# Attention, mixture of experts and FFN on one core: a third PSUM bank for the down products, a shorter 64-bit decode, and side work moved inside the units

## The chip, the cores and the metric

The kernel runs on 1 core of one Trainium2 chip. The metric is device microseconds of an execution, the median of several runs; lower is better. Before the change it is 2050.29 us (median of 3 runs, 2049.09 to 2053.37).

## The reference, cut to what matters

```python
# attention: 4 batches, 8 heads, 576 positions, head_dim 64
scores = where(mask, q @ k.T / 8, -1e9)       # heads 0-3: last 32 keys, heads 4-7: every 32nd key
x = softmax(scores) @ v                       # -> 2304 tokens x 512
# mixture of experts, E = 8, F = 1024: every token goes through every expert
P = exp(x @ w_gate - max); 8 rounds of row and column normalisation (Sinkhorn)
x = sum_e P[:, e] * (relu(x @ w1[e]) @ w2[e])
# FFN: 512 -> 2048 -> 512; its weights reach the chip as 64-bit numbers
h = x @ w_in;  out = (h * sigmoid(1.702 * h)) @ w_out
```

## The kernel before, in words

**Units.** The 2304 tokens are 3 blocks of 768 (2 x 384). A unit is one block with 256 of the hidden columns: 32 units a block in the mixture (8 experts x 4), 8 a block in the FFN, 120 in all, numbered 0 to 119. Units 0 to 31 are block 0 of the mixture, 32 to 95 blocks 1 and 2, 96 to 119 the FFN. Attention runs in front of and between units 0 to 9.

**Products.** The up product of a unit is a Strassen-like scheme of 7 products (the table `PRODUCTS`, called k = 0 to 6 here), each of 6 matmuls of 384 columns, since each fp32 factor is split into a high and a low part (high*high + high*low + low*high). Product k=0 opens PSUM bank A; 2, 4 and 6 go on adding into it; 1 opens bank C and 5 adds into it; 3 opens bank B. `product_and_after` hangs work on each: ScalarE copies A and C (line 820), VectorE adds a copy to a bank (lines 849 and 868; the one at 868 reads A after k=4, so k=6, which adds into A, has to wait for it). From the sums come the four quadrants of the hidden tile. In block 0, `activate` makes a high part on ScalarE (830) and a low part on VectorE (833). In blocks 1 and 2, `scaled` multiplies by the gate's rows on VectorE (910), with a high part on ScalarE (899) and a low part on VectorE or GpSimd (904).

**Down products.** Between two up products stands one down product of the unit (or pair of units) before. In block 0 and the FFN it is `tile_down`: 6 matmuls of 512 columns into a bank `y`, drained by VectorE into `acc` (1066 to 1072, 1080, 1082). Its first tile of a unit needs the quadrants 11 and 12 of the unit before, and 12 comes out of the late product k=5. In blocks 1 and 2 it is `chain`: 6 matmuls of 384 columns into `y`, drained by VectorE into `sum` (965, 967). `y` has two banks; so have A, B and C from unit 8 on (the lists `late` and `turn_of` in `open_bank`).

**Pieces.** The order is written out by hand. A unit is 13 pieces: up products at even ones, down products at odd ones. `side[g]` holds functions that are issued behind piece g; `spread` lays a list evenly over a range of pieces. All engines and the DMA queue of SyncE take their work in that order. Side work is:
- splits of weights into high and low parts (`split_into`: high on ScalarE at 236, low at 230 on VectorE or GpSimd, then a store so that later blocks can load them), with offsets in pieces for the low part and the store
- sums of weight quarters for the scheme: of w1 on GpSimd (215 to 217), of w2 in `plan_down_sums` (304), in line on GpSimd, or `again` on VectorE for the units before the late stage, whose w2 is loaded a second time (`raws`, line 313)
- at block changes the low parts of the next block's inputs (`input_low`, 499) and `join_sums` (988), which puts seven sums together to a block's result
- `decode`: 64 chunks of 64-bit weights, each a load, eight VectorE operations (419 to 428), one on GpSimd and a store, spread over units 34 to 90
- `plan_ahead`: splits of the first FFN units, in units 69 to 91, from one buffer `ws` with the parts `raw`, `sums` and `kw`.

At unit 32 the pool of block 0's weights is closed and `load_rows` (891) fetches the gate's rows for block 1.

## Time and profile before

| | |
|---|---|
| median of 3 runs | 2050.29 us |
| the profiled execution's own time | 2049.3 us |
| its span, first to last instruction | 2047.5 us |
| TensorE (PE) busy | 1972.0 us, 96% |
| PE weight loads | 1803.3 us, 88% |
| VectorE (DVE) | 1673.2 us, 82% |
| GpSimd (POOL) | 1202.5 us, 59% |
| ScalarE (ACT) | 817.4 us, 40% |
| DMA, HBM read and written | 383.99 and 161.53 MB, mean 268 GB/s |

PE's matmuls are pipelined and the ends of their records are modelled: one of 384 columns reads as 339 ns, while they start much closer together. So the busy share of PE hides short waits. What a stretch lost is better read from the number of its matmuls and the distance at which they start where nothing waits.

### The profile page before, as it was taken

Reading aid. Unit: us, or ns where it says so; the run is one execution under the profiler, and the core shown is the slowest. Engines: PE = TensorE matmul, PEld = TensorE weight load, DVE = VectorE, ACT = ScalarE, POOL = GpSimd, SP = SyncE. Lnnn points to the kernel's source line nnn. Section 1 sums busy time; section 2 is a strip of 40 time slices with the busy share of each in tenths; the row PEclk is TensorE's granted clock in tenths of the full one; section 3 lists DMA queues with packets and bytes.
Section 4 is the critical chain, followed back from the end, with each engine's and each line's share of the span. In section 5 each row is a group of like instructions: output and inputs, shape, how many; then the busy total and the mean of one; then the engine's idle time right before and its main releaser. Section 6 shows DMA issues by size and latency. Waiting matters only on the chain.

```text
span 2047.5 us, 33968 instructions
## 1 busy us (share of the span) xinstructions
PE 1972.0 (96%) x10865; PEld 1803.3 (88%) x10865; DVE 1673.2 (82%) x3077; ACT 817.4 (40%) x2040; POOL 1202.5 (59%) x1166
## 2 busy tenths in 40 slices
PE   8999989999999999999999999999998999999999
PEld 6777778888888899999999998989898989888887
DVE  6777688899987799999998799999997676666656
ACT  6555434545554333333333323323232335533432
POOL 4443356776877576676667767777676756800200
PEclk9999999999999999999999999999999999999999
DMA  6457588999997888988888788988888866665663
GB/s 235 137 206 243 173 277 320 366 353 344 368 350 247 285 293 289 292 288 284 281 268 286 249 300 278 297 295 301 307 303 285 273 215 229 246 229 180 211 192 127
DMA packets 294497, 547.80 MB, mean 268 GB/s; under 512 B 30672, under 2 KB 75952, under 8 KB 293040
## 3 DMA queue, kind: packets, MB, share of 16 engines
q1 hardware_dynamic: 294032, 545.18, 78.2%
q8 instruction: 87, 1.43, 0.3%
q14 instruction: 90, 0.74, 0.1%
q10 hardware_dynamic: 288, 0.46, 0.1%
HBM read 383.99 MB, written 161.53 MB: 266 GB/s over the span
## 4 chain that ended last, share of the span: by engine, by line
PE 64%; DVE 20%; DMA 8%; issue 3%; POOL 2%; ACT 2%; SPq 0%; DVEq 0%; ACTq 0%; POOLq 0%
PE pA L794 16%; PE y L957 14%; PE pC L794 8%; PE y L1055 6%; PE y L1053 6%; PE y L1054 6%; PE pB L794 4%; DVE r L910 2%; DVE comb L904 2%; DMA w<-s1moe 2%; DVE sum L967 2%; DMA s7moe<-kw 1%; PE sc L570 1%; DMA w<-s7moe 1%; DMA s2ffn<-ws 1%
## 5 line engine op out<-in xcount | busy, mean ns | idle before, releaser
L794 PE MATMUL pA<-xc,w 128*128 128x384 f32 x2880 | 581.7, 339 | 14.6 <-DVE pB L868 9.6
L957 PE MATMUL y<-comb,w 128*128 128x384 f32 x2688 | 547.8, 339 | 21.3 <-DVE sum L967 19.9
L794 PEld LDWEIGHTS pA<-xc,w 128*128 128x128 f32 x2880 | 511.0, 190 | 35.5 <-DVE pB L868 14.7
L957 PEld LDWEIGHTS y<-comb,w 128*128 128x128 f32 x2688 | 472.7, 189 | 38.8 <-DVE sum L967 36.4
L904 POOL TENSOR_TENSOR comb<-s,comb 128x384 fp32r<-128x384 f32 x256 | 285.8, 1127 | 217.7 <-ACT comb L899 210.5
L794 PE MATMUL pC<-xc,w 128*128 128x384 f32 x1464 | 297.5, 338 | 0.0
L899 ACT ACTIVATE comb<-r 128x384 fp32r<-128x384 f32 x192 | 100.9, 526 | 451.5 <-DVE r L910 418.1
L1053 PE MATMUL y<-w,hh 128*128 128x512 f32 x672 | 269.3, 401 | 9.0 <-DVE acc L1072 4.8
L1055 PE MATMUL y<-w,hl 128*128 128x512 f32 x672 | 270.1, 402 | 7.3 <-DVE hl L833 7.1
L967 DVE TENSOR_TENSOR sum<-y,sum 128x384 f32<-128x384 f32 x420 | 229.9, 548 | 51.9 <-PE y L957 50.9
L794 PEld LDWEIGHTS pC<-xc,w 128*128 128x128 f32 x1464 | 259.1, 188 | 9.8 <-issue 0.7
L1054 PE MATMUL y<-w,hh 128*128 128x512 f32 x672 | 267.2, 398 | 0.0
L230 POOL TENSOR_TENSOR w<-raw,w 128x512 fp32r<-128x512 f32 (+1 forms) x100 | 117.6, 1180 | 155.3 <-ACT w L236 136.8
L820 ACT ACTIVATE c<-pA 128x384 f32<-128x384 f32 x236 | 115.0, 487 | 184.4 <-PE pA L794 182.2
L1055 PEld LDWEIGHTS y<-w,hl 128*128 128x128 f32 x672 | 127.1, 189 | 42.1 <-DVE hl L833 14.1
L1053 PEld LDWEIGHTS y<-w,hh 128*128 128x128 f32 x672 | 127.5, 190 | 32.9 <-ACT hh L830 6.4
L929 POOL TENSOR_TENSOR s<-r,r 128x384 f32<-128x384 f32 x126 | 138.2, 1117 | 11.7 <-DVE r L910 11.7
L1082 DVE TENSOR_TENSOR acc<-y,acc 128x512 f32<-128x512 f32 x126 | 86.4, 686 | 69.8 <-PE y L1055 69.4
L794 PE MATMUL pB<-xc,w 128*128 128x384 f32 x708 | 142.8, 336 | 0.0
L1054 PEld LDWEIGHTS y<-w,hh 128*128 128x128 f32 x672 | 127.4, 190 | 15.5
L899 ACT ACTIVATE comb<-s 128x384 fp32r<-128x384 f32 x256 | 131.4, 513 | 7.8 <-POOL s L929 7.1
L794 PEld LDWEIGHTS pB<-xc,w 128*128 128x128 f32 x708 | 125.0, 188 | 4.9 <-issue 0.3
(155 smaller groups left out, 2987.7 us busy)
## 6 DMA issues: line engine op xcount, KB each, us to landing
w<-s1moe SPq DMA_DIRECT2D x448, 256.0 KB, 4.8
w<-s7moe SPq DMA_DIRECT2D x448, 256.0 KB, 4.7
s1moe<-w SPq DMA_DIRECT2D x216, 256.0 KB, 4.8
w<-s1ffn SPq DMA_DIRECT2D x133, 256.0 KB, 2.8
s7moe<-kw SPq DMA_DIRECT2D x128, 256.0 KB, 4.9
s7moe<-w SPq DMA_DIRECT2D x96, 256.0 KB, 3.8
w<-s2ffn SPq DMA_DIRECT2D x38, 512.0 KB, 4.1
raw<-wa SPq DMA_DIRECT2D x32, 512.0 KB, 6.1
```

Source lines behind the costliest of these rows:

```text
L230: eng.tensor_tensor(out=t[:, 1, :], in0=src, in1=f(t[:, 0, :]), op=ALU.subtract)
L794: nc.tensor.matmul(out=o, lhsT=w[:, hw, kk * P : (kk + 1) * P], rhs=x[:, hx, kk, :], start=opens and m == 0, stop=ends and m == len(todo) - 1,
L820: nc.scalar.activation(out=t, in_=bank[b][:, :NH], func=AF.Copy)
L899: nc.scalar.activation(out=t[:, 0, :], in_=part[i, q], func=AF.Copy)
L904: eng.tensor_tensor(out=t[:, 1, :], in0=part[i, q], in1=f(t[:, 0, :]), op=ALU.subtract)
L929: g.tensor_tensor(out=part[i, q], in0=part[i, a], in1=part[i, b], op=op)
L957: nc.tensor.matmul(out=o, lhsT=t[:, hw, dt * P : (dt + 1) * P], rhs=x[:, hx, :], start=(n == 0), stop=(n == 5))
L967: nc.vector.tensor_tensor(out=a, in0=o, in1=a, op=ALU.add)
L1053: nc.tensor.matmul(out=y, lhsT=hh[:, c], rhs=w[:, 0], start=(m == 0), stop=False)
L1054: nc.tensor.matmul(out=y, lhsT=hh[:, c], rhs=w[:, 1], start=False, stop=False)
L1055: nc.tensor.matmul(out=y, lhsT=hl[:, c], rhs=w[:, 0], start=False, stop=(m == 1))
L1082: nc.vector.tensor_tensor(out=a, in0=y, in1=a, op=ALU.add)
```

## The change

- `open_bank`: bank C keeps one bank in the late stage; the freed one is a third bank for the down products (`down_bank`), used every third time.
- `split_w1`: the low part of k=6's weights is issued 5 pieces behind its high part (was 1), the store 7 (was 3). `split_w2`: low part 2 or 1 pieces later (was 0), store 4 (was 2).
- `plan_down_sums`: sums in line at pieces 3, 3, 4, 5 (were 6, 6, 7, 7), in unit 31 at 0, 1, 1, 2; `again` at pieces 5 to 8 (were 8 to 11); splits at 6 to 9, in unit 31 at 4 to 7 (were 8 to 11), `again` at 0 to 3 of the next unit (were 0, 2, 4, 6). Nine units are done `again`, in units 11, 13, ... 27 (were eight, in 10 to 26).
- `decode`: without the operations at 421 and 427.
- `scaled`: the low part of quadrant 12 goes to GpSimd in all units of blocks 1 and 2 (was: in every second).
- block changes: three of the `input_low` in two halves, a piece or two later; `join_sums` in halves, in another order, one of them moved to GpSimd, the first already in the unit before.
- `plan_ahead`: parts rotate through `kw` and `sums`; the low part 1 piece behind the high one, stores 3 (were 0 and 4).
- the pools for blocks 1 and 2 are opened 4 pieces earlier.

```diff
-        if late and turn_of[b] % 2:
-            pool, tag = late[0], b + "2"
-        elif not late and i % 2:
+        if late:
+            if b != "C" and turn_of[b] % 2:
+                pool, tag = late[0], b + "2"
+        elif i % 2:
+    def down_bank(name):
+        turn_of["y"] += 1
+        if late and turn_of["y"] % 3 == 0:
+            return late[0].tile([P, D], F32, tag="y3", name=name)
+        return ps.tile([P, D], F32, tag="y", name=name, bufs=2)
...
-            split_into(t, src, kept, nc.vector, 1, 3)
+            split_into(t, src, kept, nc.vector, *((5, 7) if PRODUCTS[k][0] == "X22" else (1, 3)))
...
-                t = r["kw"].rearrange("p (h c) -> p h c", h=2)
+                t = r["kw"] if ft == 0 else r["sums"].rearrange("p q c -> p (q c)")
+                t = t.rearrange("p (h c) -> p h c", h=2)
...
-            lambda: v.scalar_tensor_tensor(xb, lo, 29, xb, ALU.logical_shift_right, ALU.bitwise_or),
...
-            lambda: v.tensor_scalar(lo, lo, 0x1FFFFFFF, None, ALU.bitwise_and),
...
-                put(last, 2 * m - 1, input_low, ph, m, v if m in low_v else g)
+                if m in low_v:
+                    put(last, 2 * m, input_low_half, ph, m, 0, v)
+                    put(last, 2 * m + 1, input_low_half, ph, m, 1, v)
+                else:
+                    put(last, 2 * m - 1, input_low, ph, m, g)
...
-            low_part(i, q, nc.gpsimd if q == "12" and (i - S0) % 2 == 0 else nc.vector)
+            low_part(i, q, nc.gpsimd if q == "12" else nc.vector)
...
-        y = ps.tile([P, D], F32, tag="y", name="y7", bufs=2)
+        y = down_bank("y7")
...
-        while done[0] < piece_at(S0 - 1, 7):
-            advance()
-        while done[0] < piece_at(S0, 2):
+        while done[0] < piece_at(S0 - 1, 11):
             advance()
         raws.close()
```

Three places where instructions move. First VectorE in unit 21, block 0, from the addition behind k=4 (before) or the down product of piece 5 (after) to the low part of quadrant 12 (`hl` from `pC`); `dsums` are the sums done again from the second load `raws`, `w` a weight's low part. Before:

```order
L868 TENSOR_TENSOR pB<-pA,c 128x384
L1096 SCALAR_TENSOR_TENSOR acc<-acc,pr 128x512
L304 TENSOR_TENSOR dsums<-raws_5641 128x256
L230 TENSOR_TENSOR w_5735<-sums,w_5735 128x256
L1072 SCALAR_TENSOR_TENSOR acc<-y,pr,acc 128x512
L833 SCALAR_TENSOR_TENSOR hl_5748<-pB,hh_5747 128x384
L304 TENSOR_TENSOR dsums<-raws_5641 128x256
L849 TENSOR_TENSOR pC<-pC,c 128x384
L304 TENSOR_TENSOR dsums<-raws_5641,dsums 128x256
L230 TENSOR_TENSOR w_5769<-sums,w_5769 128x256
L1072 SCALAR_TENSOR_TENSOR acc<-y,pr,acc 128x512
L833 SCALAR_TENSOR_TENSOR hl_5783<-pC,hh_5782 128x384
```

And now (the row `hl_5768<-pC` answers to the last one above):

```order
L312 TENSOR_TENSOR dsums<-raws_5619,dsums 128x256
L887 TENSOR_TENSOR pB<-pA,c 128x384
L1123 SCALAR_TENSOR_TENSOR acc<-acc,pr 128x512
L312 TENSOR_TENSOR dsums<-raws_5619,dsums 128x256
L238 TENSOR_TENSOR w_5719<-sums,w_5719 128x256
L1099 SCALAR_TENSOR_TENSOR acc<-y,pr,acc 128x512
L852 SCALAR_TENSOR_TENSOR hl_5735<-pB,hh_5734 128x384
L868 TENSOR_TENSOR pC<-pC,c 128x384
L1099 SCALAR_TENSOR_TENSOR acc<-y,pr,acc 128x512
L852 SCALAR_TENSOR_TENSOR hl_5768<-pC,hh_5767 128x384
```

Between the addition on `pC` and the low part made from it stood a sum and a weight's low part; now only the drain of `y` stands there. Two of the four sums are further up, in front of what is shown.

Second the DMA queue of SyncE at the end of unit 31 and the start of unit 32; `w` from `s1moe` are weight loads, `kw` the stores of split w2 sums, `rows` the gate's rows. Before:

```order
L234 DMA s7moe<-kw 128x512 x3
L262 DMA w_7774<-s1moe 128x512
L234 DMA s7moe<-kw 128x512
L262 DMA w_7786<-s1moe 128x512
L891 DMA rows<-prd 128x6x128
L262 DMA w_7804<-s1moe 128x512
```

And now:

```order
L242 DMA s7moe<-kw 128x512 x2
L270 DMA w_7732<-s1moe 128x512
L242 DMA s7moe<-kw 128x512 x2
L910 DMA rows<-prd 128x6x128
L270 DMA w_7787<-s1moe 128x512
```

The rows moved ahead of the two weight loads of unit 33; the last stores of `kw` still stand in front of them.

Third VectorE in a unit of block 1, over one chunk of the decode (`x` and `w` with equal numbers). Before:

```order
L421 SCALAR_TENSOR_TENSOR x_10919<-w_10918,x_10919 128x256
L849 TENSOR_TENSOR pC<-pC,c 128x384
L910 SCALAR_TENSOR_TENSOR r_11228<-pC,rows 128x384
L967 TENSOR_TENSOR sum_8090<-y_11233,sum_8090 128x384
L423 TENSOR_SCALAR w_10918<-w_10918 128x256
L910 SCALAR_TENSOR_TENSOR r_11251<-pA,rows 128x384
L967 TENSOR_TENSOR sum_8090<-y_11253,sum_8090 128x384
L424 SCALAR_TENSOR_TENSOR x_10919<-w_10918,x_10919 128x256
L426 TENSOR_SCALAR w_10918<-x_10919 128x256
```

And now:

```order
L868 TENSOR_TENSOR pC<-pC,c 128x384
L929 SCALAR_TENSOR_TENSOR r_11194<-pC,rows 128x384
L435 TENSOR_SCALAR w_10889<-w_10889 128x256
L986 TENSOR_TENSOR sum_8095<-y_11197,sum_8095 128x384
L929 SCALAR_TENSOR_TENSOR r_11217<-pA,rows 128x384
L986 TENSOR_TENSOR sum_8095<-y_11219,sum_8095 128x384
L436 SCALAR_TENSOR_TENSOR x_10890<-w_10889,x_10890 128x256
L438 TENSOR_SCALAR w_10889<-x_10890 128x256
```

The operation in front of `pC` is gone; the others keep their order between the drains of `y`, a little thinner.

## Rows read from the trace of the kernel before

**Rows 1.** The page, part 1: busy us, share of the span, instructions.
```profile
PE 1972.0 (96%) x10865; PEld 1803.3 (88%) x10865; DVE 1673.2 (82%) x3077; ACT 817.4 (40%) x2040; POOL 1202.5 (59%) x1166
```

**Rows 2.** Windows: stretch, us, busy by engine (instructions), PE clock, DMA share, GB/s.
```profile
278.66:322.70 44.04, 37.94 (x168) 32.76 (x168) 40.19 (x102) 17.39 (x47) 21.65 (x25) 0.88 0.72 247
322.70:652.96 330.26, 320.37 (x1562) 280.94 (x1562) 293.56 (x479) 169.21 (x432) 252.23 (x266) 0.99 0.97 346
652.96:686.86 33.90, 29.24 (x145) 25.98 (x145) 16.24 (x27) 11.95 (x25) 14.16 (x15) 0.90 0.59 192
686.86:1085.91 399.05, 397.09 (x2270) 392.59 (x2269) 369.33 (x692) 127.79 (x272) 273.93 (x261) 1.00 0.88 291
1085.91:1182.45 96.54, 90.75 (x506) 88.54 (x505) 76.70 (x122) 33.90 (x68) 73.76 (x61) 0.98 0.78 253
1182.45:1646.33 463.88, 439.62 (x2437) 424.67 (x2437) 416.40 (x736) 148.41 (x320) 334.07 (x319) 0.99 0.86 294
1646.33:1674.23 27.90, 23.99 (x128) 23.35 (x127) 20.87 (x34) 10.44 (x20) 9.78 (x8) 0.94 0.59 189
1674.23:2047.50 373.27, 369.35 (x1831) 329.31 (x1830) 233.77 (x403) 147.71 (x312) 100.92 (x85) 1.00 0.61 203
```

**Rows 3.** Windows of stretches without waits: units 28 and 29; 66 matmuls of unit 55.
```profile
589.62:620.90 31.28, 31.28 (x158) 28.12 (x158) 26.06 (x43) 16.73 (x43) 26.54 (x29) 1.00 0.92 315
1003.24:1014.67 11.43, 11.43 (x67) 11.43 (x67) 10.43 (x22) 3.67 (x8) 6.55 (x7) 1.00 0.71 223
```

**Rows 4.** Timeline, unit 13's last products: start us, us, instruction [idle before <-releaser].
```profile
354.97 0.88 DVE L230 TENSOR_TENSOR w<-sums,w 128x256 fp32r<-128x256 f32 x1
...
356.44 0.54 DVE L833 SCALAR_TENSOR_TENSOR hl<-pC,hh 128x384 fp32r<-128x384 f32 x1
...
357.03 0.50 PE L1055 MATMUL y<-w,hl 128*128 128x512 f32 x1 [0.42 <-DVE hl L833]
```

**Rows 5.** DMA issues of units 10 to 31: KB each, median us to landing.
```profile
raws<-wb SPq DMA_DIRECT2D x8, 512.0 KB, 6.1
```

**Rows 6.** Timeline, unit 32: the gate's rows, their first reader, PE's wait.
```profile
661.15 0.44 SPq L891 DMA_DIRECT2D rows<-prd  x1
...
669.47 0.56 DVE L910 SCALAR_TENSOR_TENSOR r<-pB,rows 128x384 f32<-128x384 f32 x1 [6.06 <-DMA rows<-prd]
...
670.74 0.79 PE L1053 MATMUL y<-w,hh 128*128 128x512 f32 x1 [3.12 <-DVE acc L1072]
```

**Rows 7.** Single lines, whole trace: ns min/median/max of one, first and last start.
```profile
L421 DVE SCALAR_TENSOR_TENSOR x<-w,x x64: 410/766/1280, 691.0 to 1556.6; 128x256 uint32<-128x256 uint32 x64
...
L427 DVE TENSOR_SCALAR w<-w x64: 283/598/1376, 697.6 to 1564.1; 128x256 uint32<-128x256 uint32 x64
...
L904 DVE TENSOR_TENSOR comb<-r,comb x160: 541/558/1444, 670.7 to 1649.7; 128x384 fp32r<-128x384 f32 x160
L904 POOL TENSOR_TENSOR comb<-r,comb x32: 999/1017/1312, 675.3 to 1634.4; 128x384 fp32r<-128x384 f32 x32
L499 DVE TENSOR_TENSOR xc<-xs,xc x6: 1072/1766/2092, 641.1 to 1646.2; 128x768 fp32r<-128x768 f32 x6
```

**Rows 8.** Waits of PE, 1182 to 1646 us: us in total, times, longest.
```profile
PE y L957 <- DVE sum L967: 12.0, 19, 1.1
PE pA L794 <- DVE pB L868: 6.6, 7, 4.4
PE pA L794 <- ACT c L820: 5.0, 2, 3.7
```

**Rows 9.** Timeline, unit 91: ScalarE on the FFN's weights, and PE behind it.
```profile
1579.61 0.63 ACT L236 ACTIVATE ws<-ws 128x512 fp32r<-128x512 f32 x1 [8.16 <-DMA s2ffn<-ws]
...
1582.53 2.29 PE L794 MATMUL pA<-xc,w 128*128 128x384 f32 x6 [4.38 <-DVE pB L868]
```

**Rows 10.** Timeline, FFN: the last read of bank C and the next k=1.
```profile
1752.18 0.56 DVE L839 TENSOR_TENSOR sg<-pC,sg 128x384 f32<-128x384 f32 x1 [0.62 <-ACT sg L838]
...
1754.86 1.21 PE L794 MATMUL pC<-xc,w 128*128 128x384 f32 x6
```

More of the change, by code (lines that the diff above doesn't have):

```diff
@@ L284, in split_w2 @@
                     kept.append((sw7[n, k].rearrange("p (h c) -> p h c", h=2), f(t)[:, :, c : c + 2 * P]))
-        split_into(t, raw[2, i][:, ft, :], kept, store=2 if i >= PLAIN else 0)
+        split_into(t, raw[2, i][:, ft, :], kept, low=(0, 2 - ft)[i >= PLAIN], store=(0, 4)[i >= PLAIN])
     down_sums = {}
@@ L308, in split @@
             src = down_sums[i][:, WHERE[PRODUCTS[k][1]][1], :]
-            split_into(t, src, sw7[n, k].rearrange("p (h c) -> p h c", h=2), eng, 0 if again is None else 1, 2)
+            split_into(t, src, sw7[n, k].rearrange("p (h c) -> p h c", h=2), eng, 1 if again is None else 2, 3)
         def load():
@@ L383, in sums, with half_of, split @@
                 r["todo"] = sums_w1(i, r["sums"])
-            def split(k, r=r, i=i, n=n):
-                t = r["kw"][:, k % 2 * 4 * P : (k % 2 + 1) * 4 * P].rearrange("p (h c) -> p h c", h=2)
+            def half_of(r, m):
+                t = r["kw"] if m < 2 else r["sums"].rearrange("p q c -> p (q c)")
+                return t[:, m % 2 * 4 * P : (m % 2 + 1) * 4 * P].rearrange("p (h c) -> p h c", h=2)
+            def split(k, m, r=r, i=i, n=n):
                 kept = sw1["ffn"][n, k].rearrange("p (h c) -> p h c", h=2)
-                split_into(t.bitcast(F32R), quarter(i, PRODUCTS[k][1]), kept, store=4)
+                split_into(half_of(r, m).bitcast(F32R), quarter(i, PRODUCTS[k][1]), kept, low=1, store=3)
             def load_again(r=r, n=n):
@@ L393, in split_again @@
             def split_again(ft, r=r, n=n):
-                t = r["kw"].rearrange("p (h c) -> p h c", h=2)
+                t = r["kw"] if ft == 0 else r["sums"].rearrange("p q c -> p (q c)")
+                t = t.rearrange("p (h c) -> p h c", h=2)
                 src = r["raw"][:, ft * D : (ft + 1) * D]
-                split_into(t.bitcast(F32R), src, sw2[n, ft].rearrange("p (h c) -> p h c", h=2), store=4)
+                split_into(t.bitcast(F32R), src, sw2[n, ft].rearrange("p (h c) -> p h c", h=2), low=1, store=3)
             tasks = [open_and_load, lambda: None, lambda: None, sums] + [lambda m=m, r=r: r["todo"][m]() for m in range(4)]
-            tasks += [lambda k=k, split=split: split(k) for k in range(NPR)]
+            tasks += [lambda k=k, m=m, split=split: split(k, m) for k, m in ((1, 0), (2, 1), (4, 0), (6, 1), (0, 2), (3, 3), (5, 0))]
             tasks += [load_again, lambda: None, lambda: None]
@@ L445, in plan_decode @@
         for i in range(len(todo) + 1):
-            for k in range(1, 10):
+            for k in range(1, 8):
                 if i < len(todo):
@@ L450, in plan_decode @@
                     order.append((i + 2, 0))
-                if k == 6 and i:
-                    order.append((i - 1, 10))
+                if k == 5 and i:
+                    order.append((i - 1, 8))
         steps = [lambda i=i, k=k: step(i, k) for i, k in order]
@@ L987, in join_sums @@
         )[n]
[L988 removed]
+        eng.tensor_tensor(out=o[:, h], in0=x[:, h], in1=y[:, h], op=ALU.add)
     def keep_z(blk):
@@ L1014, in plan_seven @@
                 put(u - 1, 3, load_rows, blk, un // UPE)
-            put(u, 6, down_input_sums, u)
-            put(u, 13, down_input_sums, u + 1)
+            for n in range(4):
+                put(u, 6, down_input_sum, u, n)
+                put(u, 13, down_input_sum, u + 1, n)
             for n, q in enumerate(DOWN[3:]):
@@ L1026, in plan_seven @@
         v, g = nc.vector, nc.gpsimd
-        engines = (v, v, g, v, v, v, g)
+        engines = (v, v, g, v, v, g, g)
         for blk in range(1, NB):
             end = FIRST_UNIT[blk + 1]
-            lo, hi = (end + 2, end + 3) if blk < NB - 1 else (end + 1, end + 3)
-            spread(
-                [lambda n=n, blk=blk: join_sums(blk, n, engines[n] if blk < NB - 1 else g) for n in (2, 0, 1, 4, 5, 3, 6)],
-                piece_at(lo, 0), piece_at(hi, 0) - 2,
-            )
-            if blk < NB - 1:
-                put(hi, 1, keep_z, blk)
+            order = (0, 1, 2, 4, 5, 6, 3) if blk < NB - 1 else (2, 0, 1, 4, 5, 3, 6)
+            todo = [
+                lambda n=n, h=h, blk=blk: join_sums(blk, n, h, engines[n] if blk < NB - 1 else g)
+                for n in order
+                for h in range(2)
+            ]
+            if blk < NB - 1:
+                side[piece_at(end + 1, 4)].append(todo.pop(0))
+                side[piece_at(end + 1, 8)].append(todo.pop(0))
+                spread(todo, piece_at(end + 2, 0), piece_at(end + 2, 12))
+            else:
+                spread(todo, piece_at(end + 1, 0), piece_at(end + 3, 0) - 2)
+            if blk < NB - 1:
+                put(end + 3, 1, keep_z, blk)
                 side[piece_at(FIRST_UNIT[PHASES.index(("ffn", blk))] - 3, 0)].append(lambda blk=blk: load_z(blk))
@@ L1046, in tile_down @@
         t = n
-        y = ps.tile([P, D], F32, tag="y", name="y", bufs=2)
+        y = down_bank("y")
         qs = ("11", "12") if t < TB // 2 else ("21", "22")
@@ L1284, in strided_attention_moe_ffn @@
             plan_sums(dp, i, piece_at(WAITING * UPE + 4 + 6 * i, 0), piece_at(WAITING * UPE + 9 + 6 * i, 0))
-        first = -(-(g - 6) // PPU)
+        first = -(-(g - 3) // PPU)
         for i in range(S0):
```

29 lines of the change are left out of this document (16 added, 13 removed).

## The prediction

> **What bounds the kernel now.** I read the page's first part, then the windows cut at the unit boundaries, then the waits of PE and the timeline around the largest of them. PE is busy for 96% of the span [rows 1], so only its waits can be won. The page hides part of them, so I count matmuls. In unit 55 66 matmuls of 384 columns take 11.43 us, 0.1732 us each, and two units of block 0 without a wait take 31.28 us [rows 3], 15.64 us each. Against these, the stretches [rows 2] lost:
> - units 10 and 11: 44.04 - 31.28 = 12.8 us (the gate's normalisation runs here)
> - units 12 to 31: 330.26 - 20 x 15.64 = 17.5 us
> - units 32 and 33: 33.90 - 15.64 - 42 x 0.1732 = 11.0 us, of which some 2.2 are transposes that stay: 8.8
> - units 34 to 60: 27 units of 84 matmuls, 2268 x 0.1732 = 392.8 of 399.05: 6.2 us
> - units 61 to 66: 504 matmuls, 87.3 of 96.54: 9.2 us
> - units 67 to 95: 2436 matmuls, 421.9 of 463.88: 42.0 us
> - unit 96: 126 matmuls, 21.8 of 27.90: 6.1 us
>
> Together 102.6 us. Behind unit 96 there is next to nothing: 23 units of 15.64 are 359.7 of 373.27 us, and the last stretch also holds the closing tiles. In front of unit 10 attention sets the time, and the change hardly touches it.
>
> Who ends the waits: VectorE nearly everywhere. It is busy for 369.33 of 399.05 us in units 34 to 60 (93%) and 416.40 of 463.88 in 67 to 95 [rows 2], and PE waits there for the drain of y, for the addition that reads A, and for ScalarE's copy [rows 8].
>
> **Units 34 to 95, the decode.** The two removed operations have medians of 766 and 598 ns, 64 of each [rows 7]: 87 us of VectorE less; at their shortest (410 and 283 ns) 44. Moving 32 low parts at 558 ns takes 18 us more off. So VectorE loses 62 to 105 us of the 862 that it is busy in units 34 to 95 [rows 2], and over some 910 us that is 83 to 88%. In 34 to 60, at 93%, the loss was only 6.2 us over 27 units; lighter than that, nearly all of it goes: I take 5.5 of 6.2. On GpSimd the 32 low parts cost 1.017 us each [rows 7], 33 us; it goes from 273.93 of 399.05 us [rows 2], 69%, to about 73%. What covers this: GpSimd makes its parts for chains of the next pair of units, a unit ahead or nearly so, and PE waited for it nowhere [rows 8].
>
> The trace shows that the two engines hold each other up: the same low part on VectorE takes 541 ns at its shortest and 1444 at its longest [rows 7]. The Trainium skill (SBUF — State Buffer, Who interferes with whom) says why: a VectorE instruction with two SBUF inputs contends with a GpSimd instruction that reads SBUF, and the one that comes second is blocked for the whole of the other. That speaks against moving the 32 low parts: by it up to 33 us of GpSimd time could hold VectorE up again, and the relief would be 29 to 72 us instead of 62 to 105. By the rows the contention is in the medians already, and the sum keeps 62 to 105.
>
> **The third bank.** With two banks a y product waits for the drain two before it, with three for the one before that: one up and one down product more, 2 x 6 x 0.1732 = 2.1 us of patience. The y waits in 67 to 95 are 12.0 us, the longest 1.1 [rows 8], so all lie inside it. But k=6 waits for line 868 with the old patience (two down products and k=5, 3.1 us), and this is the longer wait [rows 8]. So the bank alone would move waits; with the decode's relief both go. Bank C pays for it with its second bank. In the FFN its last read ends at 1752.74 us and k=1 starts at 1754.86 [rows 10]: 2.1 us spare, and this order is not changed. In block 0 PE needs the low part that reads C ahead of that k=1 anyway. I cost it at nothing; if the reads came more than 2.1 us later, PE would pay the rest in every unit.
>
> **Units 67 to 95, the FFN's weights.** ScalarE stood 8.16 us for a store, since the second half of w_out's part reuses the buffer of the first, and PE lost 4.38 us, then ran six matmuls in 2.29 us [rows 9], where it takes 1.2 at the full clock. Three such places hold 5.0 us of waits on ScalarE's copy [rows 8] and these 4.38; with the slow matmuls behind them about 14 us. The buffers now alternate, and this is gone. The other 28 us are VectorE late: 24 of them go. Taken: 38 of 42.0.
>
> **Block 0, units 12 to 31.** Most waits are the first down tile of a unit for quadrant 12's low part. In unit 13 a weight's low part of 0.88 us stands in front of it, and PE waits 0.42 us [rows 4]; this instruction is moved behind, and the sums done again, too. The timeline has a wait of this kind at the start of two units in three, on this low part or the high part in front of it; with the slow clock behind the longest I count 16 of the 17.5 us to them. New: the sums now follow the down product of piece 5, about 8.2 us into the unit (three up products, three down products, a drain), and wait in VectorE's queue for a load that takes 6.1 us in the median [rows 5] and is issued 0 to 6 us into the unit. Behind them stand the additions on B and A and the drains. DMA is 97% busy here [rows 2], so it comes no sooner. VectorE then idles 0 to 4 us, nine times; PE's patience of 3 banks and of k=6 (3.8 us here) covers part. VectorE is at 89% (293.56 of 330.26) and more once PE is faster, so the rest may surface at the unit's end. I take 0.7 us each, 6 us; bounds 0 and 27. Net 10, from -11 to 16.
>
> **Units 10 and 11.** Four sums leave unit 10 and the low part at its end goes later; the first long wait, for the gate's chain on VectorE, stays with its slow clock (0.88 over the stretch [rows 2]). Taken 4 of 12.8, bounds 0 and 7.
>
> **Units 32 and 33.** The gate's rows are issued at 661.15 and read at 669.47; PE waits until 670.74 [rows 6], and the stretch's clock of 0.90 [rows 2] adds some 3 us. The issue moves ahead of two weight loads and unit 31's sums come 5 to 6 pieces earlier, but GpSimd is full in unit 31 (four input parts, two weights, four sums, four splits), so I expect the issue 3 to 5 us earlier, which leaves 0 to 1.5 us of the wait. With the other wait of 1 us, for an input part of 1.77 us [rows 7] in front of the addition on C, now halved and behind it: taken 5.8 of 8.8, bounds 2 and 8.
>
> **Block changes, 61 to 66 and 96.** Halves of the inputs' low parts and of the joins, with three banks, replace pieces of 1.8 to 2.1 us; a half of 384 columns takes 0.56 us alone, so two halves cost at most 0.2 us more than the whole. The decode pauses here, so nothing else presses. Taken 7 of 9.2 and 4 of 6.1; bounds 4 to 11 together. In unit 96 four sums still stand in front of two drains.
>
> Sum: 4 + 10 + 5.8 + 5.5 + 7 + 38 + 4 = 74.3. I take off 4 for the added GpSimd work and the twelve or more extra instructions at block changes: 70 us. The profiled time of 2049.3 becomes 1979; it lies 1 us under the median of 2050.29, so the forecast is 1980.
>
> **Rivals.**
> 1. *The second load binds block 0.* DMA at 97% is a bound of its own: if the loads come 4 us late nine times, PE gains nothing there or loses. For: the load takes 6.1 us, and the sums come three pieces earlier. Against: the stores that held SyncE's queue come later now. Price: up to 21 us of the sum: 1990 to 2001.
> 2. *VectorE's relief is only the uncontended part*, the waits moving to k=6, which the third bank doesn't help. For: GpSimd does more, and most of an operation's time is contention (766 against 410 ns). Against: even 44 us is more than the waits. Price: half of the 24, of the 5.5 and of the block changes' 11, 20 us: 2000.
> 3. *Slower: the single bank C.* If its last read slips behind k=1's start, PE waits in each of the 109 units from 11 on. To turn 70 us into a loss takes more than 0.65 us each on top of the 2.1 spare: reads 2.8 us later than now. It would give 2055 or more. Nothing in the order puts work in front of these reads; in block 0 work leaves.
>
> **How the numbers follow.** My forecast, 1968 to 1992: 68%. Rival 1: 14%. Rival 2: 14%. Rival 3: 2%; more gained than counted (all bounds good, 86 us, 1964): 2%. The range takes the forecast and most of both rivals: 1966 to 2003. A difference of 0.2%, 4 us, is about what can be told from no change here. Faster 0.96, same 0.01, slower 0.03.
>
> **What would show it.** Right: in the profile after, VectorE at 83 to 88% in units 34 to 95, hardly a y or A wait there, no ScalarE wait for a store of s2ffn, 29 units of 14.55 us each in about 426 us; units 12 to 31 in about 320 us; no wait over 1.5 us in unit 32, and a granted clock above 0.97 there. Wrong: VectorE idle on the load raws in units 11 to 27 with PE behind it; waits on line 868's successor as long as now; a k=1 that waits for VectorE's read of C; a part from GpSimd that PE waits for.

## The result, and the profile after

The changed kernel takes 2032.9 us (median of 4 runs, 2031.87 to 2035.22) against 2050.88 for the kernel before (4 runs, 2049.09 to 2053.37): a ratio of 0.9913 with a 95% interval of 0.9896 to 0.993. That is 18 us or 0.9% faster, and the interval lies clear of 1. The forecast was 70 us, and 2033 lies above its range, too.

The profiled execution of the changed kernel spans 2030.1 us. First the page's engine line (busy us, share of the span, instructions; it answers to [rows 1]):

```profile
PE 1960.0 (97%) x10865; PEld 1800.8 (89%) x10865; DVE 1610.9 (79%) x2937; ACT 817.5 (40%) x2040; POOL 1233.5 (61%) x1201
```

Then the windows at the same unit boundaries as [rows 2] (stretch, us, busy us by engine and instructions, granted PE clock, DMA share, GB/s): units 10 and 11, 12 to 31, 32 and 33, 34 to 60, 61 to 66, 67 to 95, 96, and 97 to the end.

```profile
286.87:328.41 41.54, 36.78 (x168) 31.77 (x168) 40.17 (x98) 16.23 (x41) 23.73 (x26) 0.92 0.68 237
328.41:688.48 360.07, 329.58 (x1562) 284.17 (x1561) 320.17 (x496) 170.98 (x444) 257.52 (x266) 0.98 0.93 325
688.48:715.15 26.67, 25.84 (x145) 23.76 (x145) 14.61 (x25) 9.96 (x20) 11.45 (x11) 1.00 0.75 246
715.15:1108.88 393.73, 393.42 (x2269) 393.10 (x2269) 326.22 (x616) 128.32 (x272) 282.32 (x275) 1.00 0.88 295
1108.88:1199.38 90.50, 88.63 (x506) 87.23 (x505) 72.36 (x120) 33.77 (x68) 74.42 (x65) 1.00 0.80 263
1199.38:1628.03 428.65, 425.27 (x2437) 421.60 (x2437) 366.22 (x662) 149.04 (x320) 352.11 (x336) 1.00 0.91 320
1628.03:1656.44 28.41, 24.02 (x127) 23.32 (x127) 20.95 (x35) 10.56 (x20) 10.61 (x9) 0.94 0.58 181
1656.44:2030.10 373.66, 369.79 (x1831) 329.23 (x1830) 234.28 (x403) 147.84 (x312) 102.49 (x92) 1.00 0.60 203
```

Subtracted from [rows 2], stretch by stretch, this is the whole result:

| units | gained, us | forecast |
|---|---|---|
| ahead of unit 10 (278.66 before, 286.87 after) | -8.2 | 0 |
| 10 and 11 | 2.5 | 4 |
| 12 to 31 | **-29.8** | **10** |
| 32 and 33 | 7.2 | 5.8 |
| 34 to 60 | 5.3 | 5.5 |
| 61 to 66 | 6.0 | 7 |
| 67 to 95 | 35.2 | 38 |
| 96 | -0.5 | 4 |
| behind it | -0.4 | 0 |

From unit 32 to the end the kernel won 53 us, where 60 was forecast. In front of unit 32 it lost 35.5, where 14 of gain was forecast. Block 0 is where the gain went. What waits there now (waits in units 12 to 31 of the changed kernel: engine, line waited for, us in total, times, longest):

```profile
POOL sums L223 <- DVE w L238: 63.0, 19, 5.5
...
DVE dsums L312 <- DMA raws<-wb: 21.8, 8, 6.4
PE pA L813 <- DVE pB L887: 20.4, 15, 5.2
...
ACT w L244 <- POOL sums L223: 13.8, 13, 1.5
...
PE y L1080 <- ACT hh L849: 9.6, 10, 1.8
```

The second and third lines are rival 1: VectorE waits for the second load, and PE's k=6 waits for the addition (line 887) that stands behind it in VectorE's queue. Unit 21 shows it once, on the timeline (start us, us, engine, instruction, idle time in front and what ended it), VectorE and then PE:

```profile
506.30 0.81 DVE L312 TENSOR_TENSOR dsums<-raws 128x256 f32<-128x256 f32 x1 [2.87 <-DMA raws<-wb]
...
510.25 0.55 DVE L887 TENSOR_TENSOR pB<-pA,c 128x384 f32<-128x384 f32 x1
...
510.86 2.35 PE L813 MATMUL pA<-xc,w 128*128 128x384 f32 x12 [1.16 <-DVE pB L887]
```

The first line is something that no rival named: GpSimd waits 63 us for VectorE before the first sum of the next weights (line 223). The same stretch, unit 22, on VectorE and on GpSimd:

```profile
517.72 0.42 DVE L238 TENSOR_TENSOR w<-sums,w 128x256 fp32r<-128x256 f32 x1
...
518.22 1.41 POOL L223 TENSOR_TENSOR sums<-raw 128x512 f32<-128x512 f32 x1 [4.40 <-DVE w L238]
```

The `w<-sums` of 0.42 us is k=6's low part, which the change issues 5 pieces behind its high part instead of 1. It reads the tile `sums`, of which there is one. So GpSimd can't write the next unit's sums before VectorE has come to it, and it stands still for 4.40 us in front of a queue that also holds low parts and the down sums.

### The profile page after: what moved, and what is told of

Its sections match the earlier page's. It is cut to its first block, busy times and chain, and to the rows that moved or that the text cites. A ratio compares the mean times of both kernels' runs of the same rounds, so it can differ in the third digit from the quotient of the medians.

```text
span 2030.1 us, 33823 instructions
## 1 busy us (share of the span) xinstructions
PE 1960.0 (97%) x10865; PEld 1800.8 (89%) x10865; DVE 1610.9 (79%) x2937; ACT 817.5 (40%) x2040; POOL 1233.5 (61%) x1201
## 4 chain that ended last, share of the span: by engine, by line
PE 74%; DVE 13%; DMA 7%; POOL 2%; issue 2%; ACT 1%; SPq 1%; DVEq 0%; POOLq 0%; ACTq 0%
PE y L976 21%; PE pA L813 20%; PE pC L813 9%; PE y L1080 5%; PE y L1082 5%; PE y L1081 5%; PE pB L813 5%; DVE w L238 2%; DMA s1moe<-w 2%; DMA raws<-wb 2%; DMA s7moe<-kw 1%; DVE hl L852 1%; PE sc L589 1%; DVE acc L1099 1%; DVE kw L238 1%
## 5 line engine op out<-in xcount | busy, mean ns | idle before, releaser
L976 PE MATMUL y<-comb,w 128*128 128x384 f32 x2688 | 538.9, 335 | 6.8 <-DVE sum L986 4.4
L923 POOL TENSOR_TENSOR comb<-s,comb 128x384 fp32r<-128x384 f32 x256 | 280.9, 1109 | 71.0 <-ACT comb L918 65.7
L923 POOL TENSOR_TENSOR comb<-r,comb 128x384 fp32r<-128x384 f32 x64 | 68.0, 1063 | 145.1 <-ACT comb L918 144.2
```

What stands on the lines that cost most here:

```text
L923: eng.tensor_tensor(out=t[:, 1, :], in0=part[i, q], in1=f(t[:, 0, :]), op=ALU.subtract)
L976: nc.tensor.matmul(out=o, lhsT=t[:, hw, dt * P : (dt + 1) * P], rhs=x[:, hx, :], start=(n == 0), stop=(n == 5))
```

## The experiments

All are compared with the kernel before by the ratio of their times (interval 95%), and with each other by the length of a stretch in their profile. Where the order in units 12 to 31 was left alone (before, decode alone, buffers alone) that length is 330.3, 330.9 and 331.8 us: differences of 2 us there tell nothing. A length is of one profiled execution, and these lie within 5 us of their medians: kernel 3's took 2005.3 us (median 2000.7), kernel 5's 1995.7 (median 2000.3). The expectations speak of what a stretch *lost*; they subtract 311.4 us from the length of units 12 to 31. 14 kernels were run, in this order of questions:

| kernel | us | ratio | units 2 to 9 | 12 to 31 | 67 to 95 |
|---|---|---|---|---|---|
| before | 2050.9 | 1 | 172.3 | 330.3 | 463.9 |
| changed | 2032.9 | 0.9913 (0.9896 to 0.993) | 179.2 | 360.1 | 428.7 |
| 1 k=6 put back | 2011.8 | 0.98 (0.9781 to 0.9819) | 171.6 | 350.1 | 429.0 |
| 2 `again` sums put back | 2019.8 | 0.9838 (0.9818 to 0.9858) | 180.8 | 346.1 | 428.8 |
| 3 both | 2000.7 | 0.9752 (0.973 to 0.9773) | 171.6 | 340.3 | 433.1 |
| 4 block 0's order put back | 2001.3 | 0.9755 (0.9732 to 0.9778) | 173.0 | 333.8 | 429.4 |
| 5 k=6 back, load earlier | 2000.3 | 0.9759 (0.9729 to 0.9789) | 173.1 | 333.3 | 428.1 |
| 6 the same, splits spread | 2005.6 | 0.9792 (0.9763 to 0.9822) | 171.6 | 344.8 | 431.5 |
| 7 k=6 back, no second load | 1994.4 | 0.9744 (0.9723 to 0.9765) | 171.5 | 332.1 | 430.2 |
| 8 k=6 late, alone in before | 2056.0 | 1.0021 (1.0005 to 1.0037) | 178.0 | 331.6 | 463.8 |
| 9 decode alone in before | 2033.0 | 0.9922 (0.9893 to 0.995) | 172.8 | 330.9 | 449.3 |
| 10 third bank alone in before | 2041.1 | 0.9954 (0.9937 to 0.9971) | 172.4 | 333.0 | 457.4 |
| 11 `plan_ahead` alone in before | 2039.6 | 0.9952 (0.9934 to 0.9969) | 172.2 | 331.8 | 448.9 |
| 12 put together | 1995.7 | 0.9744 (0.9725 to 0.9764) | 173.0 | 336.3 | 429.2 |
| 13 the same, k=6 at 3 | 1998.0 | 0.974 (0.9725 to 0.9754) | 172.7 | 338.5 | 430.4 |
| 14 changed, k=6 at 3, load earlier | 2000.9 | 0.9757 (0.9743 to 0.9772) | 174.6 | 340.3 | 427.7 |

### 1 to 4: which edit harms block 0

Theory A is rival 1 (the load), theory B the held `sums` buffer. Kernel 1, in `split_w1`:

```diff
-split_into(t, src, kept, nc.vector, *((5, 7) if PRODUCTS[k][0] == "X22" else (1, 3)))
+split_into(t, src, kept, nc.vector, 1, 3)
```

> The changed kernel, with one thing put back: the low part and the store of the k = 6 gate product's weights stand 1 and 3 pieces after their high part again (5 and 7 in the changed kernel). Theory B (the late low part holds the single `sums` buffer, GpSimd waits for VectorE at L223 and its later weight sums come late; that wait is 63.0 us in 19 pieces in the changed kernel): units 2 to 9 give back their 7 us and units 12 to 31 some 15 to 25 of their 29, so 2003 to 2011 us, and the L223 wait is under 10 us. Theory A (the second load `raws` comes too late for the sums at pieces 5 to 8): block 0 stays as slow as it is, 2026 to 2033 us.

Kernel 2, in `plan_down_sums` (for `again`, also the low part at 1 and the store at 2):

```diff
-at = ... else piece_at(again, 5 + m)
+at = ... else piece_at(again, 8 + m)
-at = ... else piece_at(again + 1, m)
+at = ... else piece_at(again + 1, 2 * m)
```

> The changed kernel, with the sums of the second load put back to pieces 8 to 11 and their splits to pieces 0, 2, 4, 6 of the unit behind (5 to 8 and 0 to 3 in the changed kernel). Theory A (VectorE waits for `raws` at L312, 21.8 us in 8 pieces, and all behind it is late): that wait is gone, units 12 to 31 give back 15 to 25 of their 29 us, 2008 to 2018 us. Theory B (the late k = 6 low part): 2026 to 2033 us, and GpSimd's wait at L223 stays near 60 us.

Kernel 3 has both edits.

> Both of the two edits before in one kernel. Theories A and B together leave nothing of the 36 us that block 0 lost, but the 16 us for tail waits are not had either: 1994 to 2004 us. If a third part (splits of the down weights, in-line sums) carries a share, it shows as the rest over 2004.

Kernel 4 puts back in addition the offsets of `split_w2` and the pieces of the in-line sums and splits, except in unit 31.

> All of block 0's order of side work put back to that of the kernel before (k = 6, the second load's sums, the down weights' low parts and stores, the in-line down sums), except in its last unit; the third bank, the six-operation decode, the GpSimd low parts, the halves and the buffers for the work ahead stay. If block 0's loss lies in its order at all, units 2 to 31 come out as before or up to 2 us better, and the 54 us gained from unit 32 on stay: 1994 to 2000 us. If the loss lies in the bank or the low parts of product 12 on GpSimd, units 12 to 31 stay 10 us or more over the kernel before: 2006 us or more.

**Both theories hold, and their harms add.** Kernel 1 is 21 us faster than the changed kernel, kernel 2 is 13, both together 32. With both put back nothing else of the order matters by much, since kernel 4 takes the same time as kernel 3. Kernels 1, 2 and 4 came out 1 to 2 us above the ranges given for them. Kernel 1 gives back 7.6 us in units 2 to 9, 3.0 in 10 and 11 and 9.9 in 12 to 31 (less there than the 15 to 25 expected). GpSimd's wait falls from 63.0 us as theory B says, and the wait for the load stays (waits in units 12 to 31 of kernel 1):

```profile
DVE dsums L312 <- DMA raws<-wb: 22.3, 8, 6.8
...
PE pA L813 <- DVE pB L887: 13.6, 6, 5.4
...
POOL sums L223 <- DVE w L238: 8.9, 12, 1.7
```

In kernel 2 it is the other way round: little is left of the wait for the load, and GpSimd's wait stays (waits in units 12 to 31 of kernel 2; `hh` is the high part of a quadrant of the hidden tile, `kw` a split w2 sum):

```profile
POOL sums L223 <- DVE w L238: 58.8, 19, 6.2
...
ACT kw L244 <- DMA s7moe<-kw: 26.8, 16, 4.0
...
ACT w L244 <- POOL sums L223: 19.3, 17, 1.8
PE y L1080 <- ACT hh L849: 16.5, 8, 5.1
...
DVE dsums L312 <- DMA raws<-wb: 4.6, 2, 3.9
```

How GpSimd's lateness reaches PE shows only in part. ScalarE waits for the late sums (third line), but on its timeline what stands behind each of these 17 waits is the copy of A, not `hh`. In front of `hh`, where PE waits longest for it (4.6, 2.5 and 5.1 us in units 15, 20 and 25), stands a split that waits for a store out of `kw`. SyncE issues the stores in order, and those of the weights' low parts that GpSimd makes hold it up for 32.9 us in kernel 2 and 27.6 in the changed kernel, but for 6.4 in kernel 3 and 7.2 in kernel 1. So in kernel 2 late stores are the likely way; no run changes them alone. In the changed kernel, where ScalarE waits no longer for `kw` stores than in kernel 1 (12.5 and 13.4 us), the way isn't shown; VectorE is busy for 320.2 us there and for 311.3 in kernel 1.

### 5 to 7: is the load only late, or too much?

Kernel 5 is kernel 1 with the load at `piece_at(again - 1, 8)` instead of `piece_at(again, 0)`, five pieces earlier; sums and splits stay where the change has them.

> The changed kernel with the k = 6 low part put back (as in the first of these experiments), and the second load `raws` issued five pieces earlier, at piece 8 of the unit ahead instead of piece 0; its sums stay at pieces 5 to 8 and the splits at 0 to 3. Theory A (only the load's lateness costs, the earlier sums themselves are a gain): no wait for `raws` over 1 us, and units 12 to 31 lose 5 to 12 us instead of 48.7, so 1980 to 1990 us, better than the 2000.7 of the kernel that undoes both. Rival (four sums on VectorE at pieces 5 to 8 stand in front of the additions on B that PE's product k = 6 and ScalarE need): PE waits for line 887 at k = 6 remain, units 12 to 31 lose 22 to 32 us, 1995 to 2005 us.

The wait for `raws` is gone from the list, and units 12 to 31 take 333.3 us instead of 350.1. By the medians the load's lateness cost 11.5 us (2011.8 to 2000.3), and kernel 3, which puts the sums back, gives 11.1; between the profiles of kernels 1 and 5 it is 16.9. The gain that theory A expected on top did not come: 2000.3 is the rival's time, for a reason that neither named. There is no wait for line 887 at k=6; ScalarE waits for the stores of split down sums instead. GpSimd, too, now waits 13.3 us for the in-line loads of w2 (1.3 in kernel 1). Waits in units 12 to 31 of kernel 5, and its timeline at the start of unit 15:

```profile
ACT kw L244 <- DMA s7moe<-kw: 33.0, 26, 4.5
...
368.74 0.42 ACT L244 ACTIVATE kw<-dsums 128x256 fp32r<-128x256 f32 x1 [4.46 <-DMA s7moe<-kw]
...
371.96 0.47 ACT L849 ACTIVATE hh<-pC 128x384 fp32r<-128x384 f32 x1
...
372.49 0.63 PE L1080 MATMUL y<-w,hh 128*128 128x512 f32 x1 [3.15 <-ACT hh L849]
```

A split takes one of five `kw` buffers and holds it until its store has landed. Behind the waiting split stands `hh`, and behind that PE. In the kernel before this wait was 12.9 us in 7 places. A sixth buffer was not tried.

Kernel 6 is kernel 5 with `again`'s splits at `2 * m` and their low parts and stores as in kernel 2.

> The kernel before this one, with the splits of the second load's sums put back to pieces 0, 2, 4, 6 (low part 1 and store 2 pieces behind). If the crowd of splits in pieces 0 to 3 delays ScalarE's high part of the first down tile (`kw` waits for a store on ScalarE, then PE for `hh` at L849), this is 3 to 8 us faster than the kernel before this one. If not, it is within 2 us of it.

A miss: 5 us slower. The likely reason, which was not tested, is that the last of the spread splits (piece 6) runs into the in-line ones (6 to 9). Kernel 7 is kernel 1 without the load:

```diff
-side[piece_at(again, 0)].append(load)
-return down_raw.get(i, raw[2, i])[:, k // 2, ...]
+return raw[2, again or i][:, k // 2, ...]
```

> The changed kernel with the k = 6 low part put back and the second load `raws` left out altogether: the sums done again read the w2 weights of the unit at hand instead (so sums of the wrong unit's weights are used; the work of the engines is the same, nine loads of 512 KB are missing). The kernel with the load five pieces earlier lost 21.9 us in units 12 to 31, of which ScalarE's waits for `kw` stores stand in front of PE's waits for `hh`. If the queue of transfers sets those waits: they fall to under half (31.0 us there) and units 12 to 31 lose under 12 us, 1982 to 1990 us. If the order of the splits sets them (eight in two tight groups, five `kw` buffers), nothing changes: 1995 to 2003 us.

The waits for `kw` stores fall from 33.0 (31.0 in the expectation, from a stretch a little shorter) only to 25.1 us, and the stretch takes 332.1 us, as with the load in time (333.3). So the nine loads are the smaller part of these waits, although DMA is at 0.96 to 0.99 in these stretches. Which of the order of the splits and the time of a store sets these waits stays open.

### 8: the late low part by itself

The edit of kernel 1 turned round, in the kernel before.

> The kernel before, with the late low part and store of the k = 6 weights (5 and 7 pieces) as its only change. By theory B (GpSimd's single `sums` buffer is held until VectorE has made that low part): units 2 to 9 lose 6 to 8 us more than before, units 12 to 31 some 5 to 12 more in spite of earlier quadrants, in all 2060 to 2072 us, and GpSimd waits for VectorE at the first weight sum for 40 us or more in units 12 to 31. If the harm needs the other moves of the change: within 4 us of before or faster by up to 8 us.

It costs 4 us, where 10 to 20 were expected. Units 2 to 9 lose 5.7 us (7.0 in the changed kernel); but units 12 to 31 take 331.6 us, no more than before. The waits in these units:

```profile
ACT w L236 <- POOL sums L215: 16.1, 14, 1.8
POOL sums L215 <- DVE w L230: 16.0, 16, 2.0
...
PE y L1055 <- DVE hl L833: 0.8, 4, 0.3
...
PE y L1053 <- DVE acc L1072: 2.7, 4, 1.0
...
PE y L1053 <- ACT hh L830: 3.6, 4, 1.8
```

PE's wait for quadrant 12's low part, 4.8 us in 10 places in the kernel before, falls to 0.8, as the prediction meant it, and yet the stretch is no shorter. GpSimd waits 16.0 us for k=6's low part. In the changed kernel that wait is four times as long, but the sums hardly come later: by the timelines they start 5.0 us into the unit here and 5.3 there, in the mean of 19 units, and ScalarE waits for them as long (16.1 and 13.8 us). GpSimd only stands ready earlier, at 2.0 us into the unit instead of 4.2, since the change moved its other work ahead. Nor does the load make the difference: kernel 2, with hardly a wait for it, has 58.8 us. So in units 12 to 31 the late low part costs next to nothing in the old order and 6 to 10 us in the changed one (kernel 2 against 3, changed against 1). SyncE waits 8.8 us for GpSimd's low parts here. Which move of the change makes the difference was not run.

In units 2 to 9 there is no second load. Here GpSimd stands 7.41 us (timeline of the changed kernel; VectorE's first line is k=6's low part). The profile names no releaser, but in each of units 3 to 9 GpSimd starts 0.13 us behind that low part. What the sums then run beside gets slower: the low part that VectorE begins at 157.15 us ends 0.28 us behind GpSimd's sum. The groups below are by line on VectorE, units 2 to 9, first of the changed kernel, then of kernel 1 (busy us, mean ns):

```profile
156.01 0.41 DVE L238 TENSOR_TENSOR w<-sums,w 128x256 fp32r<-128x256 f32 x1
...
156.56 1.35 POOL L223 TENSOR_TENSOR sums<-raw 128x512 f32<-128x512 f32 x1 [7.41 <-issue]
...
157.15 1.04 DVE L238 TENSOR_TENSOR w<-raw,w 128x256 fp32r<-128x256 f32 x1
```
```profile
L238 DVE TENSOR_TENSOR w<-raw,w 128x256 fp32r<-128x256 f32 x24 | 14.8, 625 | 0.0
```
```profile
L238 DVE TENSOR_TENSOR w<-raw,w 128x256 fp32r<-128x256 f32 x24 | 10.7, 454 | 0.0
```

The same 307 VectorE instructions are busy for 140.4 us in these units of the changed kernel and 130.5 in kernel 1. PE's transposes for attention (`pt`) wait 7.9 us for VectorE's copies there (5.2 and 2.7), and about 3 in kernel 1 and in the kernel before.

### 9 to 11: who won units 34 to 95

Kernel 9 is the kernel before without the two VectorE operations of `decode`.

> The kernel before, with the six-operation decode alone (two VectorE operations a chunk less). If VectorE's relief is what won the 45 us of units 34 to 95: units 34 to 60 lose under 1.5 us (5.5 before) and units 67 to 95 some 15 to 22 of 41.2 (the waits for the s2ffn store stay, some 14 us), 2020 to 2032 us. If it takes the bank, too: units 67 to 95 lose 30 or more, 2035 to 2045 us.

Kernel 10 is the kernel before with `down_bank`, and one bank for C.

> The kernel before, with the third bank of the down products alone (C keeps one). If, as the prediction said, the bank alone only moves waits from the down products to k = 6: within 5 us of before, 2045 to 2055 us, and y <- sum waits in units 67 to 95 (12.0 us) go while the waits for line 868's successor at k = 6 grow. If it wins by itself: 2025 to 2040 us. If bank C's single buffer binds: over 2060 us, with waits at k = 1.

Kernel 11 is the kernel before with the buffers and the order of `plan_ahead`.

> The kernel before, with the buffers and the order of `plan_ahead` alone changed (parts rotate through `kw` and `sums`). If the three waits of PE for ScalarE's copy in units 76, 84 and 91 with the slow matmuls behind them are the price of the buffer that waits for its store, as the prediction has it (14 us): units 67 to 95 lose 25 to 30 us instead of 41.2, 2035 to 2041 us. If those waits only move to another engine: 2045 to 2052 us. Together with the decode alone (14.5 us less there) and the bank alone (6.4 us less there), this should make up the 35.2 us that the whole change won in that stretch.

In units 67 to 95 they win 14.6, 6.5 and 15.0 us, 36.1 together; the whole change wins 35.2. There the three add, each with its own waits, and leave next to nothing for GpSimd's low parts, which were not run by themselves. PE's waits in units 67 to 95 of kernels 9, 10 and 11 in turn, with [rows 8] for the kernel before:

```profile
PE pA L792 <- ACT c L818: 7.2, 2, 4.0
PE y L955 <- DVE sum L965: 5.0, 8, 1.3
PE pA L792 <- DVE pB L866: 3.3, 2, 3.1
```
```profile
PE pA L802 <- DVE pB L876: 16.2, 12, 3.2
```
```profile
PE y L961 <- DVE sum L971: 10.5, 17, 1.1
```

The decode leaves ScalarE's waits for stores; `plan_ahead` removes these (no wait for `c`) and leaves the drains; the bank removes the drains and moves PE to k=6 (6.6 us before, 16.2 now). In units 34 to 60 they don't add: the bank alone wins all that is to be had (393.27 us, against 393.73 in the changed kernel and 399.05 before), and the decode alone 3.5 us. In block 0 the bank wins nothing (333.0 us). Kernel 9 came out 1 us over its range: units 34 to 60 lost 2.0 us instead of under 1.5, and units 67 to 95 lost 26.7 instead of 15 to 22, since the three units with waits for stores (76, 84 and 91) cost 17.4 us where 14 had been put aside. Kernel 10 came out between two of its cases, kernel 11 as expected. Of the 7.2 us gained in units 32 and 33 none of these three holds more than 1.2, of the 6.0 in 61 to 66 none more than 3.6; the earlier issue and the halves, to which the prediction gave them, were not run alone.

### 12 to 14: the ends of the units, and a better version

Kernel 12 is kernel 4 with the load five pieces earlier and `again`'s sums at pieces 5 to 8, and in `plan_seven`:

```diff
-put(u, 13, down_input_sum, u + 1, n)
+put(u, 13 + (n if s == pairs - 1 else 0), down_input_sum, u + 1, n)
```

> A version put together from the runs so far: the changed kernel with block 0's order as before (k = 6, down weights, in-line sums, spacing of the splits), but the sums of the second load at pieces 5 to 8 and that load five pieces earlier; and in unit 96 the four sums on VectorE one down product apart instead of all four in front of one drain. If the earlier sums free the ends of units 12 to 31 once the load is in time and the splits stay spread: those units lose 8 to 14 us instead of 22.4, unit 96 2 to 3 us instead of 6.5, 1983 to 1991 us. If the ends of the units stay as late as before for another reason: 1995 to 1999 us, 4 us of it from unit 96.

Unit 96 falls from 28.41 (also in kernel 4, without this edit) to 22.99 us, at a granted clock of 1.00. Its cause in the changed kernel is on VectorE's timeline: four sums in a row, and the drain (line 986) behind them, for which PE waits 4.15 us. First the changed kernel, VectorE and PE, then VectorE in kernel 12:

```profile
1632.50 2.55 DVE L948 TENSOR_TENSOR s<-r,r 128x384 f32<-128x384 f32 x2
...
1637.50 1.47 DVE L986 TENSOR_TENSOR sum<-y,sum 128x384 f32<-128x384 f32 x3
...
1638.10 1.78 PE L976 MATMUL y<-comb,w 128*128 128x384 f32 x6 [4.15 <-DVE sum L986]
```
```profile
1601.96 1.27 DVE L948 TENSOR_TENSOR s<-r,r 128x384 f32<-128x384 f32 x1
1603.15 1.01 DVE L986 TENSOR_TENSOR sum<-y,sum 128x384 f32<-128x384 f32 x2
1604.08 1.39 DVE L948 TENSOR_TENSOR s<-r,r 128x384 f32<-128x384 f32 x1
```

But units 12 to 31 take 336.3 us, not better than in kernel 4. So the earlier sums don't free the ends of the units even when the load is in time. PE still waits for quadrant 12's low part (5.9 us in 12 places), with a weight's low part in front of it, as in [rows 4]. Kernel 13 moves that one behind quadrant 12's, but ahead of GpSimd's next sums:

```diff
-split_into(t, src, kept, nc.vector, 1, 3)
+split_into(t, src, kept, nc.vector, *((3, 5) if PRODUCTS[k][0] == "X22" else (1, 3)))
```

> The version put together before (1995.7 us, 25.0 us lost in units 12 to 31), with one change: the low part of the k = 6 weights 3 pieces behind its high part, the store 5 (1 and 3 there, 5 and 7 in the changed kernel). At 3 it stands behind the low part of quadrant 12 on VectorE, and still ahead of GpSimd's next sums, which need its buffer. If that one instruction is what stands in front of quadrant 12 and the harm of the changed kernel is only in holding the `sums` buffer: the waits of PE for the low part at L852 (8.05 us) fall under 2 us, GpSimd's wait at L223 stays under 15 us, units 12 to 31 lose 12 to 18 us, 1983 to 1990 us. If any later place of it holds GpSimd up: units 2 to 9 lose over 22 us again, 2000 us or more.

It does what it should, and wins nothing (338.5 us). Waits of PE in units 12 to 31, of kernel 12 and then of kernel 13:

```profile
PE y L1082 <- DVE hl L852: 5.9, 12, 0.7
PE y L1080 <- ACT hh L849: 5.5, 8, 1.5
PE pA L813 <- DVE pB L887: 2.7, 3, 1.8
```
```profile
PE y L1080 <- ACT hh L849: 7.7, 10, 1.5
PE pA L813 <- DVE pB L887: 4.7, 9, 1.9
```

The wait for `hl` is gone and GpSimd hardly waits (0.4 us); waits for `hh` and k=6 have taken its place. Kernel 14 has the same offset, but otherwise the order of the changed kernel, tight splits included.

> The changed kernel with three edits: k = 6's low part and store at 3 and 5 (5 and 7), the second load five pieces earlier, unit 96's sums one down product apart. All else as changed, the tight splits (0 to 3, 6 to 9) too. If the tight splits are what keeps ScalarE waiting for `kw` stores and PE for `hh`: 2 to 6 us slower than the kernel before this one, with L244's waits for s7moe stores over 23 us against under 22. If the tail gain and the splits are independent, both lose what the sum says: units 12 to 31 about 17 us, 1988 to 1994 us.

It is 2.8 us slower than kernel 13; the lengths (340.3 against 338.5) are too near to tell. ScalarE's waits for `kw` stores are 29.7 us, but 27.3 in kernel 13, so it isn't shown that the tight splits set them. What differs is GpSimd's wait for k=6's low part: 25.8 us, and 0.4 in kernel 13 with the same offset. As in kernel 8, the order around a late low part decides how long GpSimd stands. The best versions are kernels 12 and 13: 2.6% under the kernel before and some 1.7% under the changed one.

## Why the prediction was wrong

**Right: everything from unit 32 to 95.** VectorE is busy for 764.8 of 912.9 us in units 34 to 95, 84% (83 to 88% forecast), units 67 to 95 take 428.7 us (426), no wait for a store of s2ffn is left, the gate's rows are issued 2.9 us into unit 32 instead of 8.2, and the granted clock of that stretch is 1.00 instead of 0.90. Units 67 to 95 fell short by 2.8 us, 61 to 66 by 1.0, together about the 4 us held back for more GpSimd work, though PE waits nowhere for GpSimd there. Rival 2 fell: VectorE is busy for 97.6 us less (62 to 105 forecast), and the waits at k=6 in units 67 to 95 fall from 6.6 to 0.9 us. Rival 3 fell: PE waits nowhere for bank C in units 12 to 31 or in the FFN. Of the third bank alone I said that it moves waits; kernel 10 shows that it does so in units 67 to 95, and that it wins 5.8 us in 34 to 60 and 6.5 in 67 to 95 nevertheless. So the 5.5 us of units 34 to 60 are right in size, but the decode, to which I gave them, wins only 3.5 by itself (kernel 9).

**Wrong, first: k=6's low part was costed at nothing.** The step is "this instruction is moved behind". I asked what it stood in front of, not who waits for it to be done. It holds the single `sums` tile, and GpSimd's next weight sums wait for that (63.0 us). In the changed kernel it costs 7.6 us in units 2 to 9, 3.0 in 10 and 11, and 9.9 in 12 to 31: 20.5 us together, and 21 by the medians of kernel 1. Alone in the kernel before it costs 4 us (kernel 8). In units 2 to 9 the sums slow VectorE down; in 12 to 31 the way from GpSimd to PE stays open in part. That is also why "attention sets the time" in front of unit 10 was wrong.

**Wrong, second: the load was under-priced.** The step is "I take 0.7 us each, 6 us; bounds 0 and 27". Kernel 5 against kernel 1 measures 11.5 us by the medians and 16.9 by the profiles, inside the bounds and two to three times what I took. VectorE's idle time came near the forecast of 0 to 4 us nine times: 21.8 us in eight places, up to 6.4. What failed is the share that PE's patience was to cover. The load itself was no slower (6.3 us in the median, 6.1 before): in eight of nine places it is issued 5.3 to 6.9 us into the unit, mostly behind a store out of `kw`, where I had 0 to 6. Two long stalls (k=6 waits of up to 5.2 us, in units 13 and 19, where the load took 9.0 and 9.9 us) carry much of it, and a mean over nine places hid them. The mechanism was rival 1, which had 14%.

**Wrong, third: the 16 us for the waits at the ends of units 12 to 31 were not there to be won.** The step is "I count 16 of the 17.5 us to them". The trace of the kernel before shows fewer (waits of PE in units 12 to 31):

```profile
PE y L1055 <- DVE hl L833: 4.8, 10, 0.7
...
PE y L1053 <- ACT hh L830: 3.1, 4, 1.3
```

Only the first line is for the low part that [rows 4] shows behind the moved instruction. Units 15 and 20 alone take 3.0 and 5.3 us more than 15.64; PE waits there 0.5 us each for that low part, but 1.7 and 2.1 us for `hh` and a drain. Unit 20 still takes 19.7 to 21.0 us in kernels 4, 5, 12 and 13. With both harms out (kernels 4, 5, 7) and even with the low part out of the way (13) these units take 332 to 338 us, never less than the 330.3 of the kernel before. Kernels 8 and 13 remove the wait for `hl`; waits for `hh`, for the drain or for k=6 follow. I took the wait that ends last for the cause; others stood next to it. VectorE was at 89% there, with ScalarE behind the `kw` stores. I gave this term no bounds of its own, though no row excluded that it was 0. What the last limit of block 0 is stays open; kernel 7 excludes the second load.

**Wrong, fourth, and small: unit 96.** I named the four sums in front of two drains and still counted 4 of 6.1 us as won. They hold nearly all of it: kernel 12 wins 5.4 us by moving them.

The sum with these sizes: 53 us from unit 32 on; up to there no gain instead of 20, less 21 for k=6 and 12 for the load: 20. 18 was measured. That these agree so well is partly luck, since by the lengths the load costs 17 instead of 12.

## What to carry to other kernels

An instruction that is moved later keeps what it reads occupied for longer: before costing such a move at nothing, ask who writes that buffer next, on which engine, and what is queued behind the writer. A wait that ends last is worth only its distance to the next one; where several waits of half a microsecond follow each other on engines that are 90% busy, removing one moves PE to the next, and the stretch without any wait is no measure of the gain. Gains add where each ends waits of its own (the decode, a bank and two buffers in units 67 to 95), and not where one of them ends all there are (units 34 to 60). What a late instruction costs hangs on the order around it: the same late low part cost 4 us in the old order and 21 in the changed one.
